# Float64 weight tiles loaded by another queue, later products with the reciprocal, and one subtraction moved to VectorE, in a block-sparse attention with a feed-forward layer

## The chip, the cores and the metric

The kernel runs on one core of a Trainium2 chip. The metric is the device time of one launch in microseconds (us), the median of several runs. The engines are named as in the profile: PE (matrix products; PEld is its weight load), DVE (VectorE), ACT (ScalarE), POOL (GpSimd) and SP (SyncE, which here only issues transfers). Each takes its instructions in the order of the program's queue for it; an instruction that waits for a semaphore holds up those behind it. A transfer (DMA) belongs to the queue of the engine that issues it.

## The reference

Batch 4, 8 heads, 768 positions, head width 64. Scores are masked by blocks of 32 positions: a band, the first and last blocks, and three sampled blocks for each block of rows. Softmax, product with v; the heads are put side by side and go through a feed-forward layer 512 -> 2048 -> 512 with a piecewise activation.

```python
scores = scale * np.matmul(q, k.transpose(0, 1, 3, 2))
scores = np.where(mask, scores, -1000000000.0)
scores = scores - np.max(scores, axis=-1, keepdims=True)
attn = np.exp(scores)
attn = attn / (np.sum(attn, axis=-1, keepdims=True) + 1e-09)
out = np.matmul(attn, v)
...
h = x @ w_in
g = np.where(h >= 1, h, np.where(h <= -1, 0.0, (h + 1) ** 2 / 4))
return g @ w_out
```

q, k and v arrive as float32, the two weight matrices as float64.

## The kernel before

**High and low parts.** Most products are made in a rounded 32-bit form (float32r). For more digits an operand is split: the high part is the rounded value, the low part is the operand less its high part. For q and k of a head (one tile `qk` of 128 x 768, q in the upper 64 partitions and k in the lower) ACT makes the high part `qkh` (`hi`, a call of `rounded`, L196), POOL the low part in place (`lo`, L228); SP copies the four halves to where the products need them (`hi_one`, `hi_two` and `lo_two`, L221, L237, L238: `KA`, `QA`, `QB`, `KB`). The load of the next head's q and k (`load_qk`, L214) needs the tile free, that is, `lo_two` landed.

**A head** (`head`) has 12 plan units, one for each pair of a half of the query columns (384) and a block of 128 keys. Ahead of it come 12 products for row maxima (`max_mm`, L267, each followed by `max_red` on DVE, L272), the maximum's transposition and its row in QA (`max_row`, L283). Then per unit two products for the scores (L303, L304), the exponential on ACT (L308) and the product with v (L333, or L335 and L336 where the exponential is split too, with the subtraction `pl`, L316, on DVE and the running sum `acc`, L323, on POOL). The first ten heads are "whole" (not split); the first eight, those of batch 0, are "wide": they use more banks of PSUM.

**Denominators.** After each half of an odd head, the sums of a pair of heads go through DRAM (`r_in`, L377 and L378), become reciprocals on DVE (`recip`, L372), go through DRAM again and are spread over 128 partitions (`r_out`, L382 and L384: tile `den`). Then DVE multiplies (`x_mul`, L387), ACT rounds (`x_hi`) and DVE subtracts (`x_lo`, L395).

**Float64 weights.** `convert` turns a tile of 128 x 512 float64 numbers into a high and a low part: `load` (L162) brings it into `raw`, a tile with two buffers; `bits` takes one pass on ACT (L168) and four on DVE (L169, L170, L172, L174, the last two read `raw`); `split` rounds on ACT and subtracts on POOL (L180). There are 16 tiles of `moe_w_in`, planned from unit CONV on, CSTEP units apart, and 16 of `moe_w_out`, three units apart, while the first feed-forward half runs. The latter go to DRAM (`w_keep`, L448) and are read back for the later batches (`w_load`, L441).

**Feed-forward.** `moe` handles half a batch (384 columns) at a time, 16 blocks of features: `l1` (L457 to L459), activation on ACT and DVE (L463 to L478), `l2` (L485 to L487). It runs beside the heads of the next batch; the last batch's runs alone.

**Order.** Every step is put into a list with a planned time, in units, by `at(time, step)`. The dictionaries P, PW (wide heads), PA and PM hold the offsets: `cl` is how far ahead of `bits` the load of a float64 tile is planned, `r2` how far behind the reciprocal's start the products are. The list is sorted by time; that order is the priority by which a scheduler, with durations of its own, lays out each engine's queue. So a queue's order is near the planned one, not the same.

Of the kernel before, what the change touches and what calls it, by code (L numbers as in the profile page):

```python
# [10 lines left out]
I32 = mybir.dt.int32  # L11
U32 = mybir.dt.uint32
AF = mybir.ActivationFunctionType
ALU = mybir.AluOpType
# [4 lines left out]
B, H, S, D = 4, 8, 768, 64  # L19
# [5 lines left out]
NP = H // 2  # L25
# [3 lines left out]
KA = 96 + T  # L29
# [8 lines left out]
def body(ctx, tc, qk_t, v, sampled_blocks, moe_w_in, moe_w_out, ind, cm, negd, ident, fold, out):  # L38
    nc = tc.nc
    pool = lambda name, bufs, **kw: ctx.enter_context(tc.tile_pool(name=name, bufs=bufs, **kw))  # L40
    cst = pool("cst", 1)
    ld = pool("ld", 1)
# [7 lines left out]
    mt = pool("mt", 2)  # L50
    op = pool("op", 1)
    wst = pool("wst", 3)
    cv = pool("cv", 1)
# [12 lines left out]
    Q_KEEP = nc.sync  # L66
    Q_W = nc.sync
    Q_OUT = nc.sync
    Q_RAW = nc.gpsimd
    Q_QK = nc.sync  # L70
    Q_V = nc.sync

    def f(ap):
        return ap.bitcast(F32)
# [12 lines left out]
    def consts():  # L87
        M = slice(64, KM)
        for i in range(SETS):
            nc.gpsimd.memset(f(QA[i][64:128 if i == 0 else 96]), 0.0)  # L90
        nc.gpsimd.memset(VW[0][:, :, 64:128], 1.0)
        nc.gpsimd.memset(VW[1][:, :, 0:64], 1.0)
        nc.vector.memset(eps, 1e-9)
        nc.vector.memset(half_c, 0.5)
        sraw = cst.tile([128, NR, 2], I32, name="sraw")
        nc.sync.dma_start(out=sraw[M], in_=sampled_blocks.bitcast(I32).rearrange("a (r w) -> a r w", w=2))
        cmt = cst.tile([128, 2 * NB], F32, name="cmt")
        nc.sync.dma_start(out=cmt[M], in_=cm)
        ef = f(cv.tile([128, 512, 2], I32, name="raw", bufs=2).rearrange("p c w -> p (c w)"))[64:KA, 0:S]
        nc.sync.dma_start(out=ef, in_=ind)  # L100
        idf = pp.tile([128, HALF], F32, name="pt")[:, 0:128]
        nc.sync.dma_start(out=idf, in_=ident)
        nc.vector.tensor_copy(out=idr, in_=idf)
        nc.vector.tensor_copy(out=KAt[0][64:KA], in_=ef)
        nc.sync.dma_start(out=nd, in_=negd.rearrange("a (t p) -> a t p", t=T))
        nc.sync.dma_start(out=sel, in_=fold)
        for i in range(1, SETS):
            rounded(nc.gpsimd, KAt[i][64:KA], ef)
        sf = cst.tile([128, NR], F32, name="sf")
        nc.vector.tensor_copy(out=sf[M], in_=sraw[M, :, 0])  # L110
        al = cst.tile([128, NB], F32, name="al")
        nc.vector.tensor_copy(out=al[M], in_=cmt[M, 0:NB])
        for r in range(NR):
            nc.vector.scalar_tensor_tensor(
                out=al[M], in0=cmt[M, NB:2 * NB], scalar=sf[M, r:r + 1], in1=al[M],
                op0=ALU.is_equal, op1=ALU.max)
        mb = cst.tile([128, NB], F32R, name="mb")
        nc.vector.tensor_scalar(out=mb[M], in0=al[M], scalar1=-1.0, scalar2=BIG, op0=ALU.add, op1=ALU.mult)
        for hf in range(2):
            cs = slice(hf * HALF, (hf + 1) * HALF)  # L120
            pm = psa.tile([128, 512], F32, name="pa")
            nc.tensor.matmul(out=pm[0:NB, 0:HALF], lhsT=mb[M], rhs=KAt[0][64:KM, cs], start=True, stop=True)
            for i in range(SETS):
                (nc.scalar.copy if i else nc.vector.tensor_copy)(out=QA[i][64:KM, cs], in_=pm[0:NB, 0:HALF])
# [24 lines left out]
    def plan_conversions():  # L149
        last = 1e9  # L150
        for t, load, bits, split in sorted(conv, key=lambda x: -x[0]):
            last = t = min(t, last - P["cd"])
            at(t - P["cl"], load)
            at(t, bits)
            at(t + P["cs"], split)

    def convert(t, src, dst, done=None):
        st = {}

        def load():  # L160
            st["raw"] = cv.tile([128, 512, 2], I32, name="raw", bufs=2)
            Q_RAW.dma_start(out=st["raw"], in_=src.bitcast(I32).rearrange("p (c w) -> p c w", w=2))  # L162

        def bits():
            raw = st["raw"]
            lo32, hi32 = raw[:, :, 0], raw[:, :, 1]
            a = st["a"] = cv.tile([128, 512], I32, name="cva", bufs=2)
            nc.scalar.activation(out=f(a), in_=f(hi32), func=AF.Abs)  # L168
            nc.vector.tensor_scalar(out=f(a), in0=f(a), scalar1=CLO, scalar2=CHI, op0=ALU.max, op1=ALU.min)  # L169
            nc.vector.tensor_scalar(out=a, in0=a, scalar1=3, scalar2=0x3FFFFFFF,  # L170
                                    op0=ALU.logical_shift_left, op1=ALU.bitwise_and)
            nc.vector.scalar_tensor_tensor(out=a, in0=hi32, scalar=-0x40000000, in1=a,  # L172
                                           op0=ALU.bitwise_and, op1=ALU.bitwise_or)
            nc.vector.scalar_tensor_tensor(out=a, in0=lo32, scalar=29, in1=a,  # L174
                                           op0=ALU.logical_shift_right, op1=ALU.bitwise_or)

        def split():
            hi, lo = dst()
            rounded(CH, hi, f(st["a"]))
            nc.gpsimd.tensor_tensor(out=lo, in0=f(st["a"]), in1=f(hi), op=ALU.subtract)  # L180
            if done:
                done()

        conv.append((t, load, bits, split))
# [13 lines left out]
    def head(i, n0, b, h, pst):  # L198

        j, e = divmod(h, 2)  # L200
        wide = i < H
        whole = i // 2 in WHOLE
        G = {**P, **PW} if wide else {**P, **PA} if i < 2 * H else P
        o0, o1 = (L, R) if e == 0 else (R, L)
        QAi, KAi = QA[i % SETS], KAt[i % SETS]
        st = {}
# [18 lines left out]
            move(QAi[0:64], st["hi"][L])  # L225

        def lo():
            nc.gpsimd.tensor_tensor(out=st["x"], in0=st["x"], in1=f(st["hi"]), op=ALU.subtract)  # L228

        def hi_two():  # L230
            st["KB"] = qk.tile([128, S], F32R, name="KB")
# [166 lines left out]
        for hf in range(2):  # L398
            for c in range(T):
                at(s, scores, hf, c)  # L400
                at(s + G["ex"], expo, c)
                if not whole:
                    at(s + G["ph"], p_hi, c)
                    at(s + G["pl"], p_lo, c)
                    at(s + G["ps"], p_sum, hf, c)
                at(s + G["lag"], values, hf, c)
                s += 1
            u = s - 1 + G["lag"]
            if whole:
                at(u + G["ow"], o_whole, hf)  # L410
            else:
                at(u + G["ot"], o_tmp)
                at(u + G["oa"], o_add, hf)
                at(u + G["al"], acc_sum, hf)
                if e:
                    at(u + G["su"], sums, hf)
                    at(u + G["de"], dens, hf)
            if e:
                y = u + (G["yw"] if whole else G["yy"])
                if whole:  # L420
                    at(y, r_in, hf)
                    y += G["r1"]
                at(y, recip, hf)
                at(y + 0.1, r_out, hf)
                y -= G["r1"]
                y += G["r2"]
                at(y + G["xm"], x_mul, hf)
                at(y + G["xh"], x_hi, hf)
                at(y + G["xl"], x_lo, hf)
# [4 lines left out]
    def moe(t0, p, b, hf, first):  # L434

        g = {}
        G = {**P, **PM} if first else P

# [67 lines left out]
        for fi in range(NF):  # L506
            u = t0 + fi * p
            if first:
                convert(u + 1.5 * p - P["co"], moe_w_out[fi * 128:(fi + 1) * 128, :], lambda fi=fi: w_dst(fi),
                        lambda fi=fi: w_keep(fi))  # L510
# [15 lines left out]


    at(TC, consts)
    for i in range(NHEADS):
        b, h = divmod(i, H)  # L530
# [4 lines left out]
    p = PER * H / (2 * NF)  # L535
# [3 lines left out]
    for fq in range(4):  # L539
        for kt in range(4):  # L540
            cs = slice(fq * 512, (fq + 1) * 512)
# [10 lines left out]


WHOLE = (0, 1, 2, 3, 4)
P = {'vw': 4.0, 'r1': 0.857, 'r2': 4.031, 'qs': 9.647, 'ks': 11.666, 'vs': 9.131, 'ld': 5, 'm0': 7.832, 'm1': 5.0, 'mr': 0.46, 'mc': 2.3, 'mt': 1.325, 'mw': 0.9, 'ex': 0.524, 'ph': 1.22, 'pl': 1.349, 'ps': 0.841, 'ow': 0.704, 'ot': 0.2, 'oa': 0.549, 'ah': 0.3, 'al': 0.578, 'su': 0.637, 'de': 1.414, 'yw': 0.799, 'yy': 2.173, 'xm': 0.774, 'xh': 1.0, 'xl': 2.518, 'gr': 0.1, 'gs': 0.279, 'gm': 0.314, 'gh': 0.934, 'gl': 1.232, 'l2': 1.494, 'l3': 0.158, 'l1': 0.121, 'cl': 3.327, 'cs': 1.705, 'cd': 1.8, 'co': 5.196, 'lag': 3.5}
PW = {'vw': 4.0, 'r1': 3.302, 'r2': 4.413, 'qs': 12.454, 'vs': 9.131, 'ld': 5, 'm0': 7.8, 'm1': 5.61, 'mr': 0.15, 'mc': 2.3, 'mt': 1.3, 'mw': 0.9, 'ex': 0.2, 'ph': 1.231, 'pl': 1.349, 'ps': 0.841, 'ow': 0.722, 'ot': 0.2, 'oa': 0.462, 'ah': 0.3, 'al': 0.578, 'su': 0.637, 'de': 1.525, 'yw': 0.813, 'yy': 2.024, 'xm': 0.516, 'xh': 1.1600000000000001, 'xl': 2.268, 'lag': 3.403}
TC = -90
H0 = 0.711
PH1 = ()
PH2 = ()  # L560
# [10 lines left out]
NHEADS = B * H  # L571
NMOE = B
PER = 2 * T
CONV, CSTEP = 6.105, 5.609
CLO, CHI = (struct.unpack("<f", struct.pack("<I", w))[0] for w in (0x38100000, 0x47EFFFFF))

_INS = ["qk_t", "v", "sampled_blocks", "moe_w_in", "moe_w_out"]
# [49 lines left out]
```

## Time and profile before

| | |
|---|---|
| median of 3 runs | 1031.86 us (1029.77 to 1033.98) |
| profiled execution | 1029.55 us, span 1027.5 us |
| PE busy | 956.7 us (93%) |
| PEld busy | 828.1 us (81%) |
| DVE busy | 751.0 us (73%) |
| ACT busy | 635.4 us (62%) |
| POOL busy | 396.0 us (39%) |
| DMA | 154.43 MB, mean 150 GB/s |

The span is the time between the first and the last instruction of the program in the profile. Head 0's scores begin at 20.9 us, head 8's at 167.2, head 12's at 304.0; the first feed-forward half begins at 170.5 us. A share of busy time is a mean over these stages, which differ: near the end PE runs alone with few instructions on the others. A row of a group of instructions gives the line, the engine, the operation, output <- inputs, how many, busy us and mean ns, and the idle time ahead of it with what ended it; a row of a wait gives us in total, how many times, and the longest.

### The profile page before, as it was taken

How to read it: one execution, taken by the hardware profiler on the slowest of the kernel's cores; microseconds unless marked ns; L12 is line 12 of the kernel's file. 1: busy time of each engine (PE TensorE's matmuls, PEld its weight loads, DVE VectorE, ACT ScalarE, POOL GpSimd, SP SyncE). 2: the span in 40 equal slices, each digit the busy share in tenths (PEclk: the TensorE clock that was granted, in tenths of full speed). 3: DMA queues.
4: the chain of work that ended last, by engine and by line, in shares of the span. 5: the costliest groups of instructions: out<-in, count | busy, mean ns of one | idle time of the engine just before them, and what ended most of it. 6: DMA issues, size and time to landing. Idle time of an engine off the chain costs nothing.

```text
span 1027.5 us, 14635 instructions
## 1 busy us (share of the span) xinstructions
PE 956.7 (93%) x4687; PEld 828.1 (81%) x4687; DVE 751.0 (73%) x1317; ACT 635.4 (62%) x1302; POOL 396.0 (39%) x347
## 2 busy tenths in 40 slices
PE   3889887998889999999999999999999999999998
PEld 2556565777778989888988888988988899899997
DVE  5877787768999787888888887888888786422222
ACT  3566565557657666766767676766667666533433
POOL 3424233236656445454545445453545444100000
PEclk9999899999999999999999999999999999999999
DMA  6656666746435555554535455554535452433433
GB/s 169 184 153 168 182 157 199 217 146 187 152 121 165 146 146 152 147 173 127 156 122 162 137 162 152 147 167 125 151 120 178 131 144 83 149 124 123 154 131 105
DMA packets 56216, 154.43 MB, mean 150 GB/s; under 512 B 9612, under 2 KB 17952, under 8 KB 56140
## 3 DMA queue, kind: packets, MB, share of 16 engines
q1 hardware_dynamic: 51492, 136.70, 44.9%
q0 software_dynamic: 4608, 16.78, 5.6%
q8 instruction: 37, 0.61, 0.2%
q14 instruction: 39, 0.32, 0.1%
q10 hardware_dynamic: 40, 0.03, 0.0%
HBM read 100.92 MB, written 14.81 MB: 113 GB/s over the span
## 4 chain that ended last, share of the span: by engine, by line
PE 60%; DVE 12%; ACT 2%; DMA 2%; issue 2%; SPq 0%; ACTq 0%
PE oa L485 7%; PE oa L487 7%; PE oa L486 7%; PE hp L457 6%; PE hp L459 6%; PE hp L458 6%; PE po L335 4%; PE pa L303 4%; PE pa L304 4%; PE po L336 4%; PE pa L267 3%; DVE mc L272 3%; DVE pl L316 3%; DMA qk<-in_qk_t_dram 2%; DVE gl L478 2%; DVE xun L387 2%
## 5 line engine op out<-in xcount | busy, mean ns | idle before, releaser
L323 POOL TENSOR_TENSOR acc<-acc,pt 128x384 f32<-128x384 f32 x176 | 198.3, 1127 | 202.4 <-ACT pt L308 184.5
L272 DVE TENSOR_REDUCE mc<-pa 128x1 f32<-128x384 f32 x384 | 202.8, 547 | 23.7 <-PE pa L267 20.9
L316 DVE TENSOR_TENSOR pl<-pt,ph 128x384 fp32r<-128x384 f32 x264 | 177.5, 672 | 36.7 <-ACT ph L196 35.8
L196 ACT CAST ph<-pt 128x384 fp32r<-128x384 f32 x264 | 135.6, 514 | 98.2 <-PE po L335 94.9
L308 ACT ACTIVATE pt<-pa 128x384 f32<-128x384 f32 x288 | 140.6, 489 | 57.3 <-PE pa L304 48.5
L267 PE MATMUL pa<-KA,QA 88*128 88x384 f32 x384 | 143.4, 390 | 28.1 <-DVE mc L272 18.5
L457 PE MATMUL hp<-x,wi 128*128 128x384 f32 x448 | 156.9, 350 | 5.3 <-DVE r L469 5.3
L485 PE MATMUL oa<-w,gh 128*128 128x512 f32 x384 | 153.6, 400 | 0.3 <-ACT gh L196 0.3
L458 PE MATMUL hp<-x,wi 128*128 128x384 f32 x448 | 152.2, 340 | 0.0
L459 PE MATMUL hp<-x,wi 128*128 128x384 f32 x448 | 151.6, 338 | 0.0
L487 PE MATMUL oa<-w,gl 128*128 128x512 f32 x384 | 151.5, 395 | 0.0
L486 PE MATMUL oa<-w,gh 128*128 128x512 f32 x384 | 150.9, 393 | 0.0
L478 DVE TENSOR_TENSOR gl<-r,gh 128x384 fp32r<-128x384 f32 x128 | 102.6, 802 | 30.6 <-ACT gh L196 28.7
L267 PEld LDWEIGHTS pa<-KA,QA 88*128 88x128 f32 x384 | 73.9, 194 | 59.9 <-DVE mc L272 35.1
L469 DVE SCALAR_TENSOR_TENSOR r<-r,hp 128x384 f32<-128x384 f32 x112 | 61.6, 550 | 74.8 <-ACT r L466 74.8
L228 POOL TENSOR_TENSOR qk<-qk,qkh 128x768 f32<-128x768 f32 x32 | 62.1, 1940 | 119.0 <-ACT qkh L196 110.3
L303 PE MATMUL pa<-QA,KA 102*128 102x384 f32 x288 | 100.8, 350 | 6.2 <-DVE mc L272 5.2
L304 PE MATMUL pa<-QB,KB 128*128 128x384 f32 x288 | 98.1, 341 | 0.0
L463 ACT ACTIVATE r<-hp,half_c 128x384 f32<-128x384 f32 x112 | 65.1, 581 | 52.8 <-PE hp L459 49.7
L335 PE MATMUL po<-ph,vn 128*128 128x384 f32 x264 | 92.0, 349 | 4.2 <-DVE xun L345 3.2
L457 PEld LDWEIGHTS hp<-x,wi 128*128 128x128 f32 x448 | 84.8, 189 | 12.3 <-DVE r L469 7.8
L336 PE MATMUL po<-pl,vn 128*128 128x384 f32 x264 | 88.8, 336 | 0.0
(99 smaller groups left out, 1720.7 us busy)
## 6 DMA issues: line engine op xcount, KB each, us to landing
w<-wo_dram SPq DMA_DIRECT2D x112, 512.0 KB
qk<-in_qk_t_dram SPq DMA_DIRECT2D x32, 384.0 KB
raw<-in_moe_w_in_dram POOLq DMA_DIRECT2D x16, 512.0 KB, 6.2
raw<-in_moe_w_out_dram POOLq DMA_DIRECT2D x16, 512.0 KB, 4.2
wo_dram<-w SPq DMA_DIRECT2D x16, 512.0 KB
lv<-in_v_dram SPq DMA_DIRECT2D x32, 192.0 KB
KA<-qkh SPq DMA_DIRECT2D x32, 192.0 KB
QA<-qkh SPq DMA_DIRECT2D x32, 192.0 KB
```

The lines of the kernel that those rows point to most:

```text
L267: nc.tensor.matmul(out=pm[:, 0:HALF], lhsT=QAi[0:KM, t * 128:(t + 1) * 128], rhs=KAi[0:KM, kh * HALF:(kh + 1) * HALF], start=True, stop=True)
L272: nc.vector.reduce_max(out=st["mc"][:, t, kh:kh + 1], in_=st.pop(("pm", t, kh))[:, 0:HALF], axis=AX.X)
L303: nc.tensor.matmul(out=ps[:, 0:HALF], lhsT=KAi[0:KA, ks], rhs=QAi[0:KA, cs], start=True, stop=False)
L308: nc.scalar.activation(out=p, in_=st.pop(("ps", c))[:, 0:HALF], func=AF.Exp, scale=SCALE)
L316: (nc.gpsimd if i < 2 * H and c in PL1 else nc.vector).tensor_tensor(out=pl, in0=st["p", c], in1=f(st["ph", c]), op=ALU.subtract)
L323: nc.gpsimd.tensor_tensor(out=st["acc", hf], in0=prev, in1=st["p", c], op=ALU.add)
L457: nc.tensor.matmul(out=hv, lhsT=wi[:, j, 0, fs], rhs=x[:, 0], start=(j == 0), stop=False)
L458: nc.tensor.matmul(out=hv, lhsT=wi[:, j, 0, fs], rhs=x[:, 1], start=False, stop=False)
L459: nc.tensor.matmul(out=hv, lhsT=wi[:, j, 1, fs], rhs=x[:, 0], start=False, stop=(j == NP - 1))
L485: nc.tensor.matmul(out=o, lhsT=gh[:, ts], rhs=w[:, 0], start=(fi == 0), stop=False)
L486: nc.tensor.matmul(out=o, lhsT=gh[:, ts], rhs=w[:, 1], start=False, stop=False)
L487: nc.tensor.matmul(out=o, lhsT=gl[:, ts], rhs=w[:, 0], start=False, stop=(fi == NF - 1))
```

## The change

- `raw` gets three buffers instead of two, its loads are issued by SP instead of POOL, and they are planned 9.0 units ahead of `bits` instead of 3.327.
- The conversions of `moe_w_in` are planned from unit 8.0 on, 5.75 apart (before: 6.105 and 5.609).
- In wide heads, `x_mul`, `x_hi` and `x_lo` are planned 2 units later, but for the last pair of heads.
- The low part of q and k is subtracted on DVE instead of POOL.

```diff
-    Q_RAW = nc.gpsimd
+    Q_RAW = nc.sync
...
-        ef = f(cv.tile([128, 512, 2], I32, name="raw", bufs=2).rearrange("p c w -> p (c w)"))[64:KA, 0:S]
+        ef = f(cv.tile([128, 512, 2], I32, name="raw", bufs=3).rearrange("p c w -> p (c w)"))[64:KA, 0:S]
...
         def load():
-            st["raw"] = cv.tile([128, 512, 2], I32, name="raw", bufs=2)
+            st["raw"] = cv.tile([128, 512, 2], I32, name="raw", bufs=3)
             Q_RAW.dma_start(out=st["raw"], in_=src.bitcast(I32).rearrange("p (c w) -> p c w", w=2))
...
         def lo():
-            nc.gpsimd.tensor_tensor(out=st["x"], in0=st["x"], in1=f(st["hi"]), op=ALU.subtract)
+            nc.vector.tensor_tensor(out=st["x"], in0=st["x"], in1=f(st["hi"]), op=ALU.subtract)
...
                 y -= G["r1"]
-                y += G["r2"]
+                y += G["r2"] + (XLATE if wide and j < NP - 1 else 0)
                 at(y + G["xm"], x_mul, hf)
                 at(y + G["xh"], x_hi, hf)
                 at(y + G["xl"], x_lo, hf)
...
-P = {..., 'cl': 3.327, 'cs': 1.705, 'cd': 1.8, 'co': 5.196, 'lag': 3.5}
+P = {..., 'cl': 9.0, 'cs': 1.705, 'cd': 1.8, 'co': 5.196, 'lag': 3.5}
...
+XLATE = 2.0
...
-CONV, CSTEP = 6.105, 5.609
+CONV, CSTEP = 8.0, 5.75
```

More of the change, by code (lines that the diff above doesn't have):

```diff
@@ L554 @@
 WHOLE = (0, 1, 2, 3, 4)
-P = {'vw': 4.0, 'r1': 0.857, 'r2': 4.031, 'qs': 9.647, 'ks': 11.666, 'vs': 9.131, 'ld': 5, 'm0': 7.832, 'm1': 5.0, 'mr': 0.46, 'mc': 2.3, 'mt': 1.325, 'mw': 0.9, 'ex': 0.524, 'ph': 1.22, 'pl': 1.349, 'ps': 0.841, 'ow': 0.704, 'ot': 0.2, 'oa': 0.549, 'ah': 0.3, 'al': 0.578, 'su': 0.637, 'de': 1.414, 'yw': 0.799, 'yy': 2.173, 'xm': 0.774, 'xh': 1.0, 'xl': 2.518, 'gr': 0.1, 'gs': 0.279, 'gm': 0.314, 'gh': 0.934, 'gl': 1.232, 'l2': 1.494, 'l3': 0.158, 'l1': 0.121, 'cl': 3.327, 'cs': 1.705, 'cd': 1.8, 'co': 5.196, 'lag': 3.5}
+P = {'vw': 4.0, 'r1': 0.857, 'r2': 4.031, 'qs': 9.647, 'ks': 11.666, 'vs': 9.131, 'ld': 5, 'm0': 7.832, 'm1': 5.0, 'mr': 0.46, 'mc': 2.3, 'mt': 1.325, 'mw': 0.9, 'ex': 0.524, 'ph': 1.22, 'pl': 1.349, 'ps': 0.841, 'ow': 0.704, 'ot': 0.2, 'oa': 0.549, 'ah': 0.3, 'al': 0.578, 'su': 0.637, 'de': 1.414, 'yw': 0.799, 'yy': 2.173, 'xm': 0.774, 'xh': 1.0, 'xl': 2.518, 'gr': 0.1, 'gs': 0.279, 'gm': 0.314, 'gh': 0.934, 'gl': 1.232, 'l2': 1.494, 'l3': 0.158, 'l1': 0.121, 'cl': 9.0, 'cs': 1.705, 'cd': 1.8, 'co': 5.196, 'lag': 3.5}
 PW = {'vw': 4.0, 'r1': 3.302, 'r2': 4.413, 'qs': 12.454, 'vs': 9.131, 'ld': 5, 'm0': 7.8, 'm1': 5.61, 'mr': 0.15, 'mc': 2.3, 'mt': 1.3, 'mw': 0.9, 'ex': 0.2, 'ph': 1.231, 'pl': 1.349, 'ps': 0.841, 'ow': 0.722, 'ot': 0.2, 'oa': 0.462, 'ah': 0.3, 'al': 0.578, 'su': 0.637, 'de': 1.525, 'yw': 0.813, 'yy': 2.024, 'xm': 0.516, 'xh': 1.1600000000000001, 'xl': 2.268, 'lag': 3.403}
 TC = -90
+XLATE = 2.0
 H0 = 0.711
```

## The prediction

> **What bounds the kernel now.** First the page's slices, to see where an engine is full and where not; then the span cut at the places where the loop over heads changes pace.
>
> ```profile
> PE   3889887998889999999999999999999999999998
> DVE  5877787768999787888888887888888786422222
> 20.90:167.20 146.30, 124.53 (x489) 87.66 (x488) 115.31 (x206) 87.40 (x181) 46.32 (x40) 0.98 0.64 176
> 206.00:304.00 98.00, 85.84 (x403) 71.40 (x401) 82.54 (x133) 61.60 (x125) 51.40 (x44) 0.98 0.45 147
> 333.80:855.00 521.20, 509.47 (x2646) 461.79 (x2646) 429.43 (x757) 358.96 (x749) 249.78 (x216) 1.00 0.51 146
> 855.00:1027.50 172.50, 168.18 (x850) 151.62 (x848) 56.17 (x104) 77.50 (x150) 11.03 (x11) 1.00 0.38 126
> ```
>
> Columns of the last four rows: stretch, its length, busy time of PE, PEld, DVE, ACT, POOL, granted clock, share and GB/s of the DMA. From 333.8 us on PE is busy for 509.5 of 521.2 us and then 168.2 of 172.5: it is the bound, and an edit on the other engines has 16 us of gaps to win at most. From 20.9 to 167.2 us (heads 0 to 7, 18.3 us each by 146.3 / 8, 1.52 us for each of a head's 12 plan units) nothing is full: PE 85%, DVE 79%, ACT 60%. A stage in which nothing is full is held by waits, so I asked for the waits of that stretch, engine by engine.
>
> ```profile
> ACT cva L168 <- DMA raw<-in_moe_w_in_dram: 28.1, 14, 4.1
> ACT cva L168 <- DMA raw<-in_moe_w_out_dram: 8.6, 3, 4.4
> DVE cva L169 <- ACT cva L168: 8.8, 6, 3.0
> DVE mc L272 <- PE pa L267: 8.7, 10, 1.9
> DVE xun L387 <- DMA den<-s: 5.2, 3, 2.0
> PE pa L267 <- DVE mc L272: 11.0, 8, 2.4
> ```
>
> (Total us, times, longest.) ACT stands for 36.7 us in front of a float64 tile that has not landed; DVE stands behind ACT for 8.8 of it; PE stands behind DVE. The timeline shows why the tile is late, and it is a ring:
>
> ```profile
> 46.08 0.58 POOL L162 DMA_DIRECT2D raw<-in_moe_w_in_dram  x1 [1.56 <-DVE cva L174]
> 50.95 0.67 ACT L168 ACTIVATE cva<-raw 128x512 f32<-128x512 f32 x1 [2.66 <-DMA raw<-in_moe_w_in_dram]
> 57.21 0.69 DVE L174 SCALAR_TENSOR_TENSOR cva<-raw,cva 128x512 int32<-128x512 int32 x1
> 60.14 0.59 POOL L162 DMA_DIRECT2D raw<-in_moe_w_in_dram  x1
> DMA to landing us min/median/max: 4.6/6.5/9.5
> ```
>
> The load is issued when the last bit step (L174) frees one of two buffers, takes 6.5 us, and the next conversion waits for it. The plan asks for it 3.327 units ahead, 5.1 us here: less than the 6.5 us it needs.
>
> **The float64 tiles: third buffer, 9 units ahead, SP queue.** 9 units are 13.7 us here, 7.2 more than a median landing. The third buffer lets this happen: conversions stand 5.75 units apart, so a tile's buffer was last read 17.25 - 9 = 8.25 units before its load is due. The ring is cut. What it gives, counted on DVE (fullest after PE, and the one PE stands behind): 8.8 us here, and in 167 to 304 us, where the w_out tiles are converted,
>
> ```profile
> DVE cva L169 <- ACT cva L168: 11.4, 6, 3.1
> ACT cva L168 <- POOL w L180: 6.6, 7, 1.5
> POOL raw L162 <- DVE cva L174: 19.4, 7, 9.4
> SPq L448 <- POOL w L180: 54.1, 11, 9.4
> ```
>
> another 11.4. There part of the lateness is POOL's: it stands up to 9.4 us in its load, with the low part L180 behind it, for which the next conversion and SP's store of w wait. The change takes that standing off POOL. So 20.2 us of DVE's waits are removable. Something else becomes late next: the waits of DVE for PE's maximum products (8.7) stay, and in-order queues hand part of a gain back. I take 60%, 12 us. Bounds: nothing, if DVE only meets its next wait earlier; and 38 us, the whole idle time of PE in these stretches (146.3 - 124.5 = 21.8, 98.0 - 85.8 = 12.2, and 4.4 between them).
>
> ```profile
> 167.20:206.00 38.80, 34.41 (x149) 27.29 (x148) 28.96 (x48) 23.04 (x46) 12.34 (x12) 0.96 0.71 214
> ```
>
> **What SP pays.** It issues 32 loads more. One of the same 512 KB costs it 0.33 us by its median, so 32 x 0.33 = 10.6 us of a queue that otherwise mostly waits:
>
> ```profile
> L441 SPq DMA_DIRECT2D w<-wo_dram x83: 319/325/1955, 311.9 to 895.9; - x83
> SPq L214 <- DMA KB<-qk: 35.5, 8, 7.4
> ```
>
> The second row (20.9 to 167.2 us) is the danger: SP stands 4.4 us a head, 7.4 at most, until the low parts have landed, and now a raw load stands behind that. Its 7.2 us margin just covers the worst. For w_out, 3 units apart, the margin of the buffer is nil (9 units ahead, 3 buffers x 3 units): each load waits on SP for the four bit steps of three tiles earlier, about 2.2 us, with the q and k copies, the denominators and the store L448 behind it. But that store comes next on SP and waits for a later step of the same old tile (54.1 us in 11 waits above), so most of it is waited anyway. I take 0, with bounds of 0 and 13 x 2.2 = 29 us, the tiles that find all buffers used.
>
> The rows beside which a rule speaks against this part: raw's packets ran in a queue of their own, and took a fifth of the engines' time there.
>
> ```profile
> q0 software_dynamic: 2548, 9.26, 22.1%
> 0.00:26.00 26.00, 10.26 (x30) 6.91 (x30) 13.38 (x34) 8.30 (x15) 8.30 (x14) 1.00 0.61 167
> 14.36 1.42 PE L267 MATMUL pa<-KA,QA 88*128 88x384 f32 x3 [4.75 <-DMA QA<-qkh]
> 5.38 0.59 SPq L221 DMA_DIRECT2D QA<-qkh  x1
> ```
>
> The Trainium skill ("DMA: Bandwidth & Descriptors", Queues, rings and completion order, and SWDGE vs HWDGE vs iDMA) says that an engine takes turns between queues, while each queue is a ring worked in order. By that rule a small copy issued behind a raw tile now waits for all of it instead of sharing; no row of before shows it, and rival C below says what it would make.
>
> **The start.** The QA copy issued at 5.38 us lands only at 14.36, where PE waits for it; the DMA moves 167 GB/s. Today one raw tile is loaded there; with the third buffer a second can go ahead of head 0's copies: 512 KB at 167 GB/s are 3.1 us. I take +3, bounds 0 (behind the copies) and +6 (two tiles).
>
> **Low part of q and k on VectorE.** Removed: 32 POOL operations; added: 32 on DVE.
>
> ```profile
> L228 POOL TENSOR_TENSOR qk<-qk,qkh x32: 1801/1850/2390, 9.5 to 813.5; 128x768 f32<-128x768 f32 x32
> L174 DVE SCALAR_TENSOR_TENSOR cva<-raw,cva x32: 616/691/2320, 15.8 to 307.1; 128x512 int32<-128x512 int32 x32
> 58.05 2.15 POOL L228 TENSOR_TENSOR qk<-qk,qkh 128x768 f32<-128x768 f32 x1 [8.30 <-ACT qkh L196]
> 58.68 2.06 DVE L174 SCALAR_TENSOR_TENSOR cva<-raw,cva 128x512 int32<-128x512 int32 x1
> 406.36 1.85 POOL L228 TENSOR_TENSOR qk<-qk,qkh 128x768 f32<-128x768 f32 x1 [1.00 <-ACT qkh L196]
> 406.73 1.90 DVE L478 TENSOR_TENSOR gl<-r,gh 128x384 fp32r<-128x384 f32 x1
> L283 DVE TENSOR_TENSOR QA<-pa,nd 6x768 fp32r<-6x768 f32 x8 | 7.6, 950 | 3.9 <-PE pa L280 3.8
> POOL qk L228 <- ACT qkh L196: 71.2, 8, 13.0
> ```
>
> The nearest DVE price for 768 elements is 0.95 us (L283). But POOL's 1.85 us are not free for DVE now: L174, 0.69 by its median, takes 2.06 when it starts under L228. That is 1.37 us lost per head. So DVE comes out ahead by 0.4 us a head: -5 us over the 12 heads before 304 us, where it counts. I take -3; bounds: +11 (12 x 0.95, no stretch was on the path) and -5. The Trainium skill ("SBUF — State Buffer", Who interferes with whom) has the rule: a DVE operation with two inputs in SBUF and a GpSimd one that reads it exclude each other for a whole instruction. The rows agree: 2.06 and 1.90 end where L228 ends plus the operation's own time. Its page "Perfetto Trace Analysis" (Optimizing Scalar/DVE Operations) draws from it that moving work between the two might not help; by that the term would be 0 and the sum 3 us higher.
>
> The price in order: DVE now stands in its queue until ACT has made the high part, where POOL stood 71.2 us in eight waits with nothing else to do. That is rival B.
>
> **Later reciprocal products.** XLATE moves product, rounding and subtraction of pairs 0 to 2 (six halves) by 2 units, 3.0 us. DVE's three waits there are 2.0 at most, 5.2 together; they should go, and their consumers start at 170 us. I take -3, bounds 0 and -5. CONV and CSTEP put the last w_in tile 4 units (6 us) later; it is used by feature block 12, planned 41 units after: 0.
>
> **After 304 us.** No conversion is left. The DVE operation stretched under L228 (406.73) is now a subtraction of 0.95: -1, within PE's gaps (16 us).
>
> Sum: -12 + 0 + 3 - 3 - 3 - 1 = -16. The profiled execution took 1029.55 us (span 1027.5), 2.3 under the median of 1031.86. 1029.55 - 16 = 1013.5; on the median's footing 1015.9. I say 1015. No change to be told from noise is 0.5%, 5.2 us: 1026.7 to 1037.
>
> **Rivals.**
> A. The waits are covered by DVE's own work: DVE needs 115 us of the 146 already, and the tiles' arrival frees only ACT. Or the planner's order issues the loads no earlier. Then the 12 shrinks to 3 or less: 1029.55 - 16 + 9 = 1022.5 to 1029. For it: PE's longest waits are for DVE. Against: DVE is idle for 31 of 146 us.
> B. Slower: L228's place on DVE. If DVE stands w us per head for ACT's high part, it costs 12w early and part of 20w later, where PE's queue runs behind DVE. The other terms are worth 16, so it is slower than before by 5 from 12w = 21, w = 1.75. POOL's 71.2 / 8 = 8.9 us bounds w, though POOL came early. At w = 2 on the first 12 and 0.6 on 20: +36, 1029.55 - 16 + 36 = 1050; at w = 1.75 in the first 12 alone 1034.5.
> C. One queue: each of some 28 raw tiles after the start puts 512 KB / 176 GB/s = 3 us before the copies behind it. If a quarter is on the path, +21: 1034.5; if one in ten, +8, 1022.
> D. The ring was all: the early stage falls to DVE's work, about 118 us with its remaining stretches, for 146, and nothing else grows: -28 and -3 later, about 999.
>
> **How the numbers follow.** Forecast 0.50 (its own range 1006 to 1024); A 0.18; D 0.15; B 0.09; C 0.08. Faster: forecast, D, a third of A and C's lighter half: 0.74, of which I give back 0.03 to unseen mixtures: 0.71; same: most of A and some of C, 0.16; slower: B and the rest of C, 0.13. The range 1000 to 1034 leaves out B's far half, part of D and of C.
>
> **What would show it.** In the changed profile: ACT's wait for raw near 0 and loads on SP 9 to 20 us before their use; heads 0 to 7 in about 136 us; no DVE operation of two inputs at 2 us beside L228, L228 at 0.95 to 1.1 on DVE; xun's wait for den gone up to 170 us; the same pace after 333 us. Wrong: waits of DVE for qkh over 1.75 us a head, a later first maximum than 17.5 us, or PE waiting for QA, QB or KB copies behind raw.

## The result, and the profile after

The changed kernel takes 991.31 us (median of 4 runs, 990.66 to 1000.32) where the kernel before took 1031.68 in the same set: a ratio of 0.9629, 95% interval 0.9597 to 0.9662. The forecast was 1015 with a range of 1000 to 1034. The sign was right, the size was 40 us instead of 16, and that is outside the range. The profiled execution took 991.61 us, span 989.8.

First the slices of the page after, then the span cut at the first score product of heads 0, 8, 9, 12 and 31, after and (the last three rows) before; columns as in the prediction.

```profile
PE   5898899999899999999999999999999999999998
DVE  5888887679998887888888897888888885422222
```

```profile
16.60:154.60 138.00, 124.32 (x491) 88.58 (x490) 119.09 (x226) 93.48 (x187) 26.22 (x19) 0.99 0.68 196
154.60:178.30 23.70, 23.41 (x110) 19.11 (x109) 16.84 (x31) 15.01 (x31) 1.30 (x1) 1.00 0.65 195
178.30:281.50 103.20, 95.62 (x438) 79.16 (x438) 86.53 (x148) 66.18 (x135) 42.06 (x34) 0.97 0.51 161
281.50:817.20 535.70, 530.87 (x2794) 489.40 (x2793) 449.03 (x823) 381.33 (x795) 239.80 (x211) 1.00 0.52 152
817.20:989.80 172.60, 167.82 (x848) 151.30 (x846) 55.83 (x104) 77.20 (x149) 10.65 (x11) 1.00 0.39 126
```

```profile
198.20:304.00 105.80, 93.64 (x439) 77.98 (x437) 87.07 (x142) 66.49 (x134) 53.50 (x46) 0.98 0.49 158
304.00:855.40 551.40, 538.88 (x2794) 487.51 (x2794) 458.51 (x806) 380.84 (x795) 267.06 (x229) 1.00 0.51 148
855.40:1027.50 172.10, 167.78 (x848) 151.31 (x846) 55.77 (x104) 77.20 (x149) 10.63 (x11) 1.00 0.38 126
```

| stage | before | after | difference | the prediction's terms |
|---|---|---|---|---|
| up to head 0's scores | 20.9 | 16.6 | -4.3 | +3 |
| heads 0 to 11 | 283.1 | 264.9 | -18.2 | -18 (-12, -3, -3) |
| heads 12 to 30 | 551.4 | 535.7 | -15.7 | -1 |
| the rest | 172.1 | 172.6 | +0.5 | 0 |
| span | 1027.5 | 989.8 | -37.7 | -16 |

The row that matters most is that of heads 12 to 30. PE was "busy" for 538.88 of 551.40 us before, that is, idle for 12.5 us. The same 2794 matrix products now take 15.7 us less: 7.7 of these were idle time (12.5 became 4.8), and 8.0 were shown as busy time, though the work is the same. The end of a matrix product is modelled in this profile, so its busy time can hide waiting. The rows of the weight loads had the gap all along; these are the two weight loads that stand ahead of maximum and score products, and four kinds of DVE operations, heads 12 to 30, before and after:

```profile
L303 PEld LDWEIGHTS pa<-QA,KA 102*128 102x128 f32 x229 | 43.1, 188 | 12.4 <-DVE mc L272 7.6 <-ACT pt L308 1.3
L267 PEld LDWEIGHTS pa<-KA,QA 88*128 88x128 f32 x228 | 42.8, 188 | 15.3 <-DVE mc L272 10.7 <-DVE rc L369 0.7
L316 DVE TENSOR_TENSOR pl<-pt,ph 128x384 fp32r<-128x384 f32 x229 | 149.8, 654 | 25.6 <-ACT ph L196 24.6
L478 DVE TENSOR_TENSOR gl<-r,gh 128x384 fp32r<-128x384 f32 x76 | 71.6, 942 | 7.9 <-ACT gh L196 6.3
L387 DVE TENSOR_TENSOR xun<-xun,den 128x384 f32<-128x384 f32 x20 | 21.7, 1086 | 2.7 <-DMA den<-s 2.5
L469 DVE SCALAR_TENSOR_TENSOR r<-r,hp 128x384 f32<-128x384 f32 x77 | 42.4, 551 | 30.5 <-ACT r L466 30.5
```

```profile
L303 PEld LDWEIGHTS pa<-QA,KA 102*128 102x128 f32 x228 | 43.0, 188 | 4.1 <-ACT pt L308 0.6
L267 PEld LDWEIGHTS pa<-KA,QA 88*128 88x128 f32 x228 | 42.8, 188 | 4.5 <-DVE mc L272 0.3
L316 DVE TENSOR_TENSOR pl<-pt,ph 128x384 fp32r<-128x384 f32 x228 | 140.8, 617 | 23.5 <-ACT ph L196 22.7
L478 DVE TENSOR_TENSOR gl<-r,gh 128x384 fp32r<-128x384 f32 x76 | 60.6, 797 | 8.1 <-ACT gh L196 6.3
L387 DVE TENSOR_TENSOR xun<-xun,den 128x384 f32<-128x384 f32 x20 | 13.7, 684 | 2.3 <-DMA den<-s 2.3
L469 DVE SCALAR_TENSOR_TENSOR r<-r,hp 128x384 f32<-128x384 f32 x77 | 42.5, 552 | 28.4 <-ACT r L466 28.2
```

27.7 us of waiting ahead of these loads, 18.3 of it for the maxima on DVE, became 8.6. The difference, 19.1 us, covers the 15.7. DVE's subtraction `gl`, which the low part on POOL used to lengthen, fell from 942 to 797 ns on average. Together with `pl` and the denominators' product (L387) it gave back 28.0 us, 1.5 a head; the low part itself put 19.1 us (19 of 1.005) on DVE. The operation L469, whose second input is in PSUM, kept its 0.55 us. The Trainium skill ("Trainium Kernel Development and Optimization", Best Practices) says to judge distance from the limit by MFU (the share of the peak rate) and the busy share of weight loads, and not by the busy share of matrix products; the rows agree: PE's busy share of the stage went from 97.7% to 99.1%, the weight loads' from 88.4% to 91.4%.

At the start, SP's queue now holds the first float64 tile back:

```profile
5.46 0.59 SPq L221 DMA_DIRECT2D QA<-qkh  x1
12.29 0.43 SPq L162 DMA_DIRECT2D raw<-in_moe_w_in_dram  x1
PE pa L267 <- DMA QA<-qkh: 2.3, 1, 2.3
```

The tile was issued at 2.93 us on POOL, ahead of head 0's copies; now it is at 12.29, behind them, and PE's wait for QA is 2.3 us instead of 4.75. That is not the whole of the 4.3 us: in only_lo, below, the tile still goes ahead, at 2.92 us, and head 0's scores begin at 17.8. What moved them there is open.

### The profile page after: what moved, and what is told of

It is laid out like the page before. It is cut to its first block, busy times and chain, and to the rows that moved or that the text cites. A ratio compares the mean times of both kernels' runs of the same rounds, so it can differ in the third digit from the quotient of the medians.

```text
span 989.8 us, 14583 instructions
## 1 busy us (share of the span) xinstructions
PE 947.2 (96%) x4687; PEld 830.4 (84%) x4687; DVE 735.9 (74%) x1349; ACT 637.2 (64%) x1302; POOL 323.5 (33%) x283
## 4 chain that ended last, share of the span: by engine, by line
PE 70%; DVE 7%; ACT 2%; issue 1%; POOL 0%; POOLq 0%; ACTq 0%; DVEq 0%
PE oa L485 8%; PE oa L487 8%; PE oa L486 8%; PE hp L457 7%; PE hp L458 7%; PE hp L459 7%; PE po L335 5%; PE pa L303 4%; PE pa L304 4%; PE po L336 4%; PE pa L267 4%; DVE pl L316 2%; DVE mc L272 1%; PE pa L459 1%; PE pa L458 1%
## 5 line engine op out<-in xcount | busy, mean ns | idle before, releaser
L323 POOL TENSOR_TENSOR acc<-acc,pt 128x384 f32<-128x384 f32 x176 | 206.6, 1174 | 189.9 <-ACT pt L308 146.2
L316 DVE TENSOR_TENSOR pl<-pt,ph 128x384 fp32r<-128x384 f32 x264 | 166.9, 632 | 33.3 <-ACT ph L196 32.4
L267 PE MATMUL pa<-KA,QA 88*128 88x384 f32 x384 | 139.4, 382 | 8.8 <-DMA QA<-qkh 5.9
L469 DVE SCALAR_TENSOR_TENSOR r<-r,hp 128x384 f32<-128x384 f32 x112 | 61.8, 552 | 74.6 <-ACT r L466 74.4
L478 DVE TENSOR_TENSOR gl<-r,gh 128x384 fp32r<-128x384 f32 x128 | 91.0, 711 | 30.2 <-ACT gh L196 28.1
L323 POOL TENSOR_TENSOR acc<-pt 128x384 f32<-128x384 f32 x44 | 45.6, 1037 | 136.7 <-ACT pt L308 132.9
```

The costliest lines, as they stand in the source:

```text
L267: nc.tensor.matmul(out=pm[:, 0:HALF], lhsT=QAi[0:KM, t * 128:(t + 1) * 128], rhs=KAi[0:KM, kh * HALF:(kh + 1) * HALF], start=True, stop=True)
L316: (nc.gpsimd if i < 2 * H and c in PL1 else nc.vector).tensor_tensor(out=pl, in0=st["p", c], in1=f(st["ph", c]), op=ALU.subtract)
L323: nc.gpsimd.tensor_tensor(out=st["acc", hf], in0=prev, in1=st["p", c], op=ALU.add)
```

## The experiments

Each row of this table is one kernel, cut as above (us; heads 12 to 30 also per head), the ratio to the kernel before, run in the same set, with its interval. Medians of different sets differ by up to 3 us for the kernel before itself, so totals are compared by ratios and stages by the traces. "Tiles" is how many float64 tiles ACT passes over between head 0's and head 8's first score product.

Two cautions on the columns. The kernels no_xlate, old_grid, short_lead and two_bufs change nothing in the late heads and have 28.07 to 28.28 us a head there, so a difference of 0.2 us is not to be read. And PE's granted clock in heads 0 to 7 was 0.98 before, 0.99 after, 0.95 in only_lo, 0.97 in lo_back, and 0.93 in only_raw and pool_queue. The missing share times the length of the stage gives an estimate of 3, 1, 7, 4, 11 and 10 us of PE's time; how much of that was on the path is not shown.

| kernel | median | ratio | to head 0 | heads 0-7 | tiles | head 8 | 9-11 | 12-30 | per head |
|---|---|---|---|---|---|---|---|---|---|
| before | 1031.68 | 1 | 20.9 | 146.3 | 18 | 31.0 | 105.8 | 551.4 | 29.02 |
| after | 991.31 | 0.9629 (0.9597 to 0.9662) | 16.6 | 138.0 | 20 | 23.7 | 103.2 | 535.7 | 28.20 |
| only_lo | 1009.34 | 0.9807 (0.9768 to 0.9846) | 17.8 | 144.5 | 18 | 29.5 | 103.5 | 537.9 | 28.31 |
| lo_back | 1016.77 | 0.9876 (0.9843 to 0.9908) | 15.1 | 147.4 | 21 | 17.8 | 110.9 | 552.7 | 29.09 |
| only_raw | 1022.38 | 0.9917 (0.9886 to 0.9948) | 15.9 | 150.5 | 21 | 17.7 | 111.7 | 553.3 | 29.12 |
| pool_queue | 999.73 | 0.9715 (0.9682 to 0.9749) | 23.9 | 141.9 | 19 | 23.6 | 100.3 | 537.0 | 28.26 |
| no_xlate | 991.83 | 0.9603 (0.9565 to 0.9642) | 15.2 | 140.0 | 20 | 23.6 | 102.0 | 536.6 | 28.24 |
| old_grid | 992.04 | 0.9620 (0.9590 to 0.9649) | 16.0 | 139.2 | 20 | 17.9 | 110.6 | 537.4 | 28.28 |
| short_lead | 993.77 | 0.9633 (0.9587 to 0.9679) | 15.1 | 139.6 | 20 | 23.7 | 103.8 | 533.4 | 28.07 |
| two_bufs | 994.44 | 0.9640 (0.9596 to 0.9684) | 16.2 | 142.4 | 20 | 18.3 | 109.3 | 536.7 | 28.25 |
| pool_reads | 1019.59 | 0.9883 (0.9847 to 0.9920) | 17.2 | 165.9 | 20 | 23.7 | 103.0 | 536.7 | 28.25 |
| pool_writes | 993.74 | 0.9631 (0.9588 to 0.9674) | 16.2 | 142.1 | 19 | 23.4 | 100.6 | 537.4 | 28.28 |
| pool_reads2 | 1012.86 | 0.9824 (0.9776 to 0.9873) | 16.7 | 142.9 | 20 | 23.7 | 104.2 | 550.4 | 28.97 |
| pool_writes2 | 995.47 | 0.9647 (0.9601 to 0.9693) | 15.1 | 141.8 | 20 | 23.7 | 102.1 | 537.2 | 28.27 |
| dve_twice | 986.28 | 0.9560 (0.9525 to 0.9595) | 21.2 | 124.5 | 16 | 27.2 | 104.8 | 535.6 | 28.19 |
| dve_twice2 | 1005.07 | 0.9752 (0.9733 to 0.9772) | 16.3 | 133.4 | 20 | 23.6 | 104.9 | 551.9 | 29.05 |
| spacers | 985.99 | 0.9564 (0.9548 to 0.9580) | 16.5 | 132.3 | 18 | 23.4 | 102.6 | 536.0 | 28.21 |

### Which part makes the late heads faster

**only_lo**, the kernel before with one line changed:

```diff
-            nc.gpsimd.tensor_tensor(out=st["x"], in0=st["x"], in1=f(st["hi"]), op=ALU.subtract)
+            nc.vector.tensor_tensor(out=st["x"], in0=st["x"], in1=f(st["hi"]), op=ALU.subtract)
```

> The kernel before with one edit: the low part of q and k on VectorE. Theory P (POOL's subtraction held DVE's two-input operations up, and PE's maximum and score products stood behind DVE): heads 12 to 30 fall from 29.0 to about 28.2 us each (-16 us), heads 0 to 11 gain 0 to 5: about 1013 us. Rival Q (the late pace came with the loads, through another order of the queues): heads 12 to 30 stay at 29.0, about 1031 us.

**lo_back**, the changed kernel with that line undone:

> The changed kernel with the low part back on POOL. Theory P: heads 12 to 30 at 29.0 us again, +16 us and up to 5 more in the early heads: 1007 to 1012 us, and two-input DVE operations of 1.9 us beside L228 again. Rival Q: late heads stay at 28.2, about 993 us.

The late pace follows this one line in both directions: 28.31 with it alone, 29.09 with everything but it. Rival Q has fallen. (lo_back's total is above the 1007 to 1012 expected; its late heads are as expected.) The line is worth 1.9% alone (1 - 0.9807) and 2.5% in the changed kernel (0.9876 - 0.9629), some 20 and 25 us: half of the whole or more. The weight-load rows and `gl` of lo_back, heads 12 to 30, are those of before again:

```profile
L303 PEld LDWEIGHTS pa<-QA,KA 102*128 102x128 f32 x228 | 42.9, 188 | 11.1 <-DVE mc L272 6.3 <-ACT pt L308 1.4
L267 PEld LDWEIGHTS pa<-KA,QA 88*128 88x128 f32 x228 | 42.8, 188 | 15.0 <-DVE mc L272 10.9
L478 DVE TENSOR_TENSOR gl<-r,gh 128x384 fp32r<-128x384 f32 x76 | 70.6, 929 | 8.9 <-ACT gh L196 7.3
```

### The lock, or POOL's time

To tell whether POOL's subtraction did harm by shutting DVE out or by keeping POOL busy, I gave POOL a useless operation per head in the changed kernel, once one that reads tiles and once memsets of about the same length. **pool_reads** and **pool_writes** had it on a scratch tile alone:

```diff
+        def extra():
+            nc.gpsimd.tensor_tensor(out=scr, in0=scr, in1=scr, op=ALU.subtract)   # pool_reads
+            for _ in range(3): nc.gpsimd.memset(scr[:, 0:640], 0.0)               # pool_writes
...
+        at(pre - G["qs"] + 0.4, extra)
```

> The changed kernel with one more POOL subtraction of 128 x 768 per head on a scratch tile of its own, at the planned time of the low part; nobody waits for it. Theory L (a POOL operation that reads two tiles shuts out DVE's two-input operations while it runs): late heads go from 28.2 back to about 29.0 us, DVE operations of 1.9 us beside it, about 1010 us. Rival O (it was POOL's time: the running sums behind it came late): the same 29.0. Rival H (it was the place of the low part in the chain from load to copy): 28.2, about 992 us.

> The changed kernel with three memsets of 128 x 640 on POOL per head instead, together about as long (1.8 us) and reading nothing. Theory L: late heads 28.2 to 28.3, about 992 us. Rival O: about 29.0 and 1010 us, as with the subtraction.

These two missed their aim. With nothing to wait for, the scheduler put all 32 operations at the beginning: those of pool_reads stand between 3.7 and 62.6 us, so the late heads (28.25, 28.28) say nothing. They say something of the early ones, where heads 0 and 1 grew from 36.4 to 61.4 us with the operations that read, and heads 0 to 7 by 4 us in all with the memsets. **pool_reads2** and **pool_writes2** tie the operation to the head by reading its high part:

```diff
+            nc.gpsimd.tensor_tensor(out=scr, in0=f(st["hi"]), in1=f(st["hi"]), op=ALU.subtract)   # pool_reads2
+            nc.gpsimd.tensor_tensor(out=scr[:, 0:8], in0=f(st["hi"][:, 0:8]), in1=f(st["hi"][:, 0:8]), op=ALU.subtract)
+            for _ in range(3): nc.gpsimd.memset(scr[:, 0:640], 0.0)                               # pool_writes2
```

> As pool_reads, but the added POOL subtraction (128 x 768, scratch output) reads the head's own high part, so that no scheduler can place it before the head it belongs to: one per head, also in heads 12 to 30. Theory L (a POOL operation that reads two tiles shuts out DVE's two-input operations): late heads 28.2 -> 29.0 us, +15 us there, operations of 1.9 us on DVE beside it; 1005 to 1012 us in all. Rival O (POOL's time, the running sums behind it come late): the same time, but without stretched operations on DVE. Rival H (the low part's place between load and copies): 28.2 and about 992.

> Three memsets of 128 x 640 per head on POOL behind a subtraction of 8 columns of the head's high part that ties them to it, about 1.9 us of POOL in all. Theory L: late heads 28.2 to 28.3, about 992 us. Rival O: late heads 29.0 and over 1005 us, as in the run with the subtraction.

From the tile view of the scratch tile and from the groups of heads 12 to 30, first pool_reads2:

```profile
L233 POOL TENSOR_TENSOR scr<-qkh x32: 1460/1469/2248, 8.6 to 795.8; 128x768 f32<-128x768 f32 x32
L273 PEld LDWEIGHTS pa<-KA,QA 88*128 88x128 f32 x228 | 43.1, 189 | 13.2 <-DVE mc L278 9.4
L484 DVE TENSOR_TENSOR gl<-r,gh 128x384 fp32r<-128x384 f32 x76 | 67.6, 889 | 8.4 <-ACT gh L198 6.9
```

then pool_writes2:

```profile
L235 POOL MEMSET scr<- x96: 632/634/794, 8.7 to 780.6; 128x640 f32 x96
L275 PEld LDWEIGHTS pa<-KA,QA 88*128 88x128 f32 x228 | 42.8, 188 | 4.7 <-DVE mc L280 0.3
L486 DVE TENSOR_TENSOR gl<-r,gh 128x384 fp32r<-128x384 f32 x76 | 60.5, 797 | 10.0 <-ACT gh L198 8.6
```

1.47 us of POOL that reads (both inputs are the high part) costs a late head 0.77 us, lengthens `gl` to 889 ns and makes PE wait for DVE's maxima. 3 x 0.634 = 1.9 us of POOL that only writes, behind a subtraction of 8 columns (0.2 us) that ties it to the head, costs 0.08 us, which is within the spread, and leaves `gl` at 797. So it was not POOL's time (rival O), nor the low part's place between load and copies (rival H: in pool_reads2 it stays on DVE); it was DVE's operations held up while POOL reads. The page of the Trainium skill that the prediction named ("SBUF — State Buffer", Who interferes with whom) says this: a DVE instruction with two SBUF inputs contends with a GpSimd one that reads, not with one that only writes.

### What the same work costs on DVE

**dve_twice** (scratch tile alone) and **dve_twice2** (tied to the high part) add a second subtraction of 128 x 768 per head on DVE:

```diff
+            nc.vector.tensor_tensor(out=scr, in0=f(st["hi"]), in1=f(st["hi"]), op=ALU.subtract)   # dve_twice2
```

> The changed kernel with a second subtraction of 128 x 768 per head on DVE, on a scratch tile: the price of the low part on DVE by itself. DVE is 86% busy in heads 0 to 7, so +0.95 us x 12 = 11 us or less before head 12; in the late heads 0 to 0.5 us each, 0 to 10 us. Total 995 to 1010 us. If a DVE operation of 0.95 us costs the late heads as much as the POOL one did (0.8 us each), length alone explains the loss and not the lock.

> As dve_twice (a second DVE subtraction of 128 x 768 per head, scratch output), but it reads the head's own high part, so that one stands in every head. Late heads: if DVE's length decides, 28.2 -> 28.5 to 29.0; if only the lock beside POOL did, and DVE has room, 28.2 to 28.3. Heads 0 to 7: DVE busy plus idle is the whole stage, so +7.6 us, unless the added operation takes the place of an idle wait as in dve_twice (then shorter than 138).

Late heads: 29.05, so the second operation (1.15 us on average) costs 0.85 us a head, as much as POOL's reading one did. DVE has room for one such operation in a late head and not for two. Three of its rows in heads 12 to 30:

```profile
L322 DVE TENSOR_TENSOR pl<-pt,ph 128x384 fp32r<-128x384 f32 x228 | 157.5, 691 | 17.3 <-ACT ph L198 15.3
L233 DVE TENSOR_TENSOR scr<-qkh 128x768 f32<-128x768 f32 x19 | 21.8, 1146 | 0.0
L282 DVE TENSOR_TENSOR mr<-mc 128x6 fp32r<-128x6 f32 x19 | 7.9, 414 | 0.0
```

This sets a limit to the lock story: what keeps DVE from the maxima costs a late head, whether it is POOL's read or DVE's own work. POOL's read held DVE for 1.37 us in the prediction's row, where the subtraction itself holds it for 0.95. The run is no clean measure of length, though. DVE's busy time in the stage grew by 36.0 us (449.03 to 485.03) and not by the 21.8 of the added operation; `pl` went from 617 to 691 ns, and the combination of the maxima (`mr`) from 151 to 414. Whether length or the place in the queue decides is open.

Early heads: dve_twice, where again all 32 operations went to the beginning (3.7 to 194 us), was to be slower and is 5 us faster than the changed kernel. This is followed up at the end.

### The float64 tiles

**only_raw** takes the kernel before and gives it SP's queue, three buffers and the lead; **pool_queue**, **short_lead** and **two_bufs** take one of the three from the changed kernel:

```diff
-    Q_RAW = nc.sync
+    Q_RAW = nc.gpsimd                     # pool_queue
-'cl': 9.0
+'cl': 3.327                               # short_lead
-name="raw", bufs=3
+name="raw", bufs=2                        # two_bufs
```

> The kernel before with SP's queue, three buffers and 9.0 units of lead for the float64 tiles, but the old grid of conversions, products as early as before, and the low part on POOL. Theory P: the early part of the gain alone, start -4, heads 0 to 11 -8 to -18, late heads 29.0: 1010 to 1020 us. Rival Q: -30 or more, about 1000 us.

> The changed kernel with the float64 tiles issued by POOL again (three buffers and the lead of 9 units kept). If lead and buffers make the early gain: within 3 us of 991. If the queue does (POOL standing in its load with the low parts L180 behind it; the first tile ahead of head 0's copies): +8 to +15 us, most of it before head 0's scores and in heads 8 to 11.

> The changed kernel with the old lead of 3.327 units for the float64 tiles, three buffers kept. If the lead of 9 units brings the tiles in time, ACT waits for raw again (10 to 25 us of waiting) and the time rises by 5 to 12 us. If the scheduler issues a load as soon as a buffer is free, whatever its planned time, the third buffer does it and the time stays at 991.

> The changed kernel with two buffers for the float64 tiles, lead 9 kept. If the third buffer cuts the ring (last bit step, load, next conversion), ACT waits some 30 us for raw in heads 0 to 7 as before, DVE's idle time there goes from 19 back to about 30 us, and heads 0 to 7 take about 145 us: +7, 998 us. If the queue and the lead are enough, 991.

Lead and third buffer can't be told from nothing by the totals: the intervals around 0.9633 and 0.9640 overlap the one around 0.9629. ACT's waits for a tile are gone in both. These are two_bufs' from 16 to 155 us, then pool_queue's in heads 0 to 7; before, they were 36.7 us:

```profile
ACT cva L168 <- DMA raw<-in_moe_w_in_dram: 0.8, 2, 0.4
```

```profile
ACT cva L168 <- DMA raw<-in_moe_w_in_dram: 3.9, 3, 2.1
ACT cva L168 <- DMA raw<-in_moe_w_out_dram: 2.5, 2, 1.8
```

In short_lead a tile of `moe_w_in` is issued 8.3 us ahead of its use (median of the starts of L162 and L168), with the lead of 9 units 9.0: the scheduler issues it about as early either way.

Of the three parts it is the queue that shows in the total: back on POOL, with lead and buffers kept, the time is 8.4 us longer. 7.3 us of it lie before head 0's scores, where now two tiles go ahead of head 0's copies, at 2.92 us (PE waits 7.6 us for QA there), and 3.9 in heads 0 to 7, where the clock (0.93 instead of 0.99) can account for them. But the queue is not the one thing that spares ACT its waits: lead and third buffer on POOL's queue bring them from 36.7 us down to 6.4. Two buffers suffice on SP's queue because a tile lands sooner there: in two_bufs it is used 6.0 us after its issue with 0.8 us of waiting in all, before 6.4 us after it with 28.1. Why it lands sooner is open; the profile does not give the landing on SP's queue itself.

And ACT's waits were not the time. In lo_back (1.1 us left) and only_raw they are gone, and heads 0 to 7 are no shorter. In only_raw the clock may hide a gain; in lo_back it was about that of before. only_raw was expected at 1010 to 1020 us with 8 to 18 won in heads 0 to 11; they won 3.2 (279.9 instead of 283.1). The length of a stage is DVE's busy time plus its idle time, and DVE is the fullest engine after PE, so that is where to look (heads 0 to 7, rows of before and after are shown above):

```profile
15.10:162.50 147.40, 130.58 (x501) 93.08 (x500) 128.60 (x223) 94.28 (x190) 41.41 (x27) 0.97 0.67 191
```

```profile
17.80:162.30 144.50, 128.33 (x490) 91.56 (x489) 112.30 (x214) 88.55 (x182) 29.53 (x32) 0.95 0.65 177
```

In lo_back (the first row) DVE's idle time is 147.4 - 128.6 = 18.8 us, before it was 31.0. But DVE is busy 13.3 us longer: 21 tiles are converted there instead of 18, and the bit passes stand beside POOL's reads. The pass L170, which has one input, shows it: its rows of lo_back and of the changed kernel in heads 0 to 7, and one case in lo_back.

```profile
L170 DVE TENSOR_SCALAR cva<-cva 128x512 int32<-128x512 int32 x21 | 17.1, 812 | 0.4
L170 DVE TENSOR_SCALAR cva<-cva 128x512 int32<-128x512 int32 x20 | 8.9, 448 | 0.4
56.53 2.27 POOL L228 TENSOR_TENSOR qk<-qk,qkh 128x768 f32<-128x768 f32 x1 [1.56 <-ACT qkh L196]
57.14 1.94 DVE L170 TENSOR_SCALAR cva<-cva 128x512 int32<-128x512 int32 x1
```

The gain is handed to head 8, which takes 17.8 us instead of 31.0, and heads 9 to 11 give 5 back. In only_lo (the second row) DVE's work falls to 112.3 and the idle time stays (32.2). The changed kernel has both, 119.1 and 18.9. By these sums heads 0 to 7 gain 8.3 us together, and 1.8 and -1.1 alone. The clock is a rival here that no run sets aside: by the estimate above only_lo lost 7 us to it, lo_back 4 and the changed kernel 1, and without these the two gains alone would add up to about the joint one.

### The products and the grid

```diff
-XLATE = 2.0
+XLATE = 0.0                               # no_xlate
-CONV, CSTEP = 8.0, 5.75
+CONV, CSTEP = 6.105, 5.609                # old_grid
```

> The changed kernel without the 2 units on the reciprocal products. By the prediction's term +3 us (0 to 5), in heads 2 to 7 alone, with DVE waiting for den again: about 994 us. Rival: the products' place costs nothing, 991 us.

> The changed kernel with the conversions on the old grid (from 6.105, 5.609 apart). If the grid is worth anything it is in heads 0 to 7 through another order on DVE: 0 to 10 us slower, 991 to 1001. By the prediction's term: 0.

Neither total can be told from the changed kernel's. DVE's wait for the denominators in heads 0 to 7 was 5.2 us before and is 1.1 after; without XLATE it is 1.6 up to 150 us. The loads and the subtraction had already moved it. The grid moves time between stages (head 8 17.9 instead of 23.7, heads 9 to 11 110.6 instead of 103.2) and leaves the sum.

### Idle time by order

**spacers** puts two useless DVE operations into each of heads 0 to 7, tied to the high part, and none later:

```diff
+            for _ in range(2):
+                nc.vector.tensor_tensor(out=scr, in0=f(st["hi"]), in1=f(st["hi"]), op=ALU.subtract)
...
+        if i < H:
+            at(pre - G["qs"] + 0.4, extra)
```

> The changed kernel with two scratch subtractions on DVE in each of heads 0 to 7 alone, tied to the head's high part. Theory W (heads 0 to 7 last as long as DVE's work plus its idle time, and the idle time comes from the planned order: DVE stands at L169 behind ACT's pass on a tile; an operation in between takes that time): heads 0 to 7 in 125 to 132 us, 980 to 986 us in all. Rival: the first run was faster for another reason (32 operations before 194 us kept conversions away), then 138 + 15 = 153 us and about 1004.

985.99 us, 5 us under the changed kernel (by the ratios 7), and heads 0 to 7 in 132.3 (expected 125 to 132): the rival's 153 has fallen. DVE's waits in heads 0 to 7 of the changed kernel, the first two of spacers, and the stage of spacers:

```profile
DVE cva L169 <- ACT cva L168: 8.1, 4, 2.5
DVE mc L272 <- PE pa L267: 4.9, 8, 1.7
DVE QA L283 <- PE pa L280: 2.3, 3, 1.1
DVE xun L387 <- DMA den<-s: 1.1, 1, 1.1
```

```profile
DVE mc L280 <- PE pa L275: 4.3, 9, 0.9
DVE cva L171 <- ACT cva L170: 1.9, 1, 1.9
```

```profile
16.50:148.80 132.30, 123.22 (x493) 89.64 (x492) 122.28 (x228) 90.45 (x182) 23.98 (x16) 0.99 0.64 188
```

DVE does 3 us more and stands idle for 10.0 instead of 18.9 us: it no longer reaches L169 before ACT's pass on the tile is done, and two tiles less are converted in these heads, without heads 8 to 11 growing (126.0 instead of 126.9). The granted clock was 0.99 in both. So some 6 us of the changed kernel's heads 0 to 7 came from its queue order. An order as good without useless operations was not tried.

## Why the prediction was wrong

- **The step that failed: "After 304 us ... -1, within PE's gaps (16 us)"**, with "an edit on the other engines has 16 us of gaps to win at most" behind it. Heads 12 to 30 won 15.7 us. The prediction took the stretched DVE operation at 406 us as one case, worth 1.90 - 0.95. Over the 19 heads the stretch came to 28.0 us, against 19.1 us of subtraction that DVE took over. And it read PE's busy time as work, so that nothing seemed to wait for DVE. The weight-load rows of the same trace had 27.7 us of waits ahead of two lines, 18.3 of them for DVE. The 16 us were not exceeded in size, but they were not the bound: of the 15.7 only 7.7 came out of PE's gaps, and 8.0 out of time shown as busy. The mechanism (L228 on POOL stretching a DVE operation that PE then waits for) stood in the prediction; it was priced for 12 heads and denied for the other 20.
- **The start, +3, was -4.3.** It was taken that a second tile would go ahead of head 0's copies. SP issued the tiles behind them (12.29 us). pool_queue shows the case that was priced: 23.9, +3.0. As only_lo starts 3.1 us earlier too, the tile is not the whole cause.
- **Heads 0 to 11, -18, measured -18.2**, but not by the terms; that the sum agreed is luck. The -12 was to be 60% of DVE's 20.2 us of waits for ACT's pass (L169). These waits are still 18.5 us after (8.1 in heads 0 to 7, 10.4 in heads 8 to 11), although ACT's own waits for the tiles are gone. DVE's idle time did fall by 12.1 us in heads 0 to 7 (31.0 to 18.9), but at its other waits: for the maximum products 8.7 to 4.9, for the denominators 5.2 to 1.1, for the row of maxima (L283) 3.8 to 2.3. The -3 for the products is 0.5 (no_xlate, not to be told from nothing). The -3 for the subtraction is -5.6 alone (only_lo, heads 0 to 11).
- **"9 units are 13.7 us here, 7.2 more than a median landing"** played no part by itself: short_lead is not slower by more than can be told, for its loads are issued about as early. The 7.2 us were also said to cover SP's longest wait, 7.4; nothing came of that.
- **Rival A** (covered by DVE's own work) came true for the loads by themselves in heads 0 to 7 and was wrong for the whole. **Rival B** has fallen: DVE's subtraction waited 0.6 us for ACT's high part, once, in 32. **Rival C** has fallen too: with one queue the time was 8.4 us shorter than with two, and PE's waits for the QA copies rose from 0.9 to 3.6 us in heads 0 to 7, no more. By the Trainium skill's rule that a ring is worked in order ("DMA: Bandwidth & Descriptors", Queues, rings and completion order) small copies should have waited behind the tiles. The rise has that direction; no run shows whether the ring made it. At the start the rule is not needed: SP had not issued the tile yet. **Rival D** (999) came nearest in time by another way: it had heads 0 to 7 at DVE's work of 118 us and 3 us won later; they took 138.0, and 15.7 were won in heads 12 to 30.
- Right: the price of the subtraction on DVE (0.95 us; measured median 0.946), the two-input operations beside L228 as its gain, SP's added issues as free, heads 0 to 7 in about 136 us (138.0), and the last stage as unmoved (+0.5).

## What to carry to other kernels

Take the gaps of a PE-bound stage from the weight loads' rows and what they wait for, not from the busy time of the matrix products. A two-input operation on POOL can hold a DVE operation with two SBUF inputs almost to its end (2.06 us instead of 0.69 beside one of 2.15), and here it held the one-input pass L170 too (1.94 instead of 0.43). So moving it to DVE can pay even where DVE is the fuller engine; price it in every stage where DVE feeds PE. Where an order of queues comes from a scheduler, a wait that is removed may be filled with work from a later stage: compare the work done per stage before saying that the edit gained nothing. An operation that is added as a test has to be tied to its place by its data, or the scheduler puts it at the beginning.

## What the runs showed of the hardware that was not expected

- The same products of heads 12 to 30 ran in 535.7 instead of 551.4 us while PE's idle time before had been 12.5 us in all: a stage shown as 97.7% busy had 2.8% to give.
- Two useless DVE operations in each early head made the whole kernel 5 us faster (spacers 985.99 against 991.31), and one in every head made it 14 us slower (dve_twice2 1005.07).
- POOL's memsets, 1.9 us a head, cost the late heads 0.08 us each, within the spread (pool_writes2); its reads of 1.47 us cost 0.77.
- Not only DVE's two-input operations were held: of the passes L170, with one input, five took 1.93 to 2.08 us in heads 0 to 7 of lo_back, each beside L228, and 0.43 us is its median there.
